# An attention segment on TensorE: four filler products per head group, with four later products brought forward and staged out of PSUM

## The chip, the cores and the metric

The kernel runs on one core of one Trainium2 chip. The metric is device time in microseconds (us) of one execution; a run's figure is the median of its executions. TensorE (PE) multiplies matrices and writes to PSUM, of which this program uses eight banks; ScalarE (ACT) computes exponentials and GELUs, VectorE (DVE) does elementwise work and statistics, GpSimd (POOL) the masks, and SyncE issues the transfers. The granted clock is the share of PE's full clock that the profile recorded as granted (1.00 on the pages of both kernels).

## The reference, cut to what matters

A pre-LayerNorm attention block with a compressive memory, followed by a gMLP block. 2048 tokens of width 1024, 32 heads of width 32, four segments of 512 tokens.

```python
for s in range(4):                                   # segments
    p = softmax(qs @ ks.T * scale + mask)            # causal, inside the segment
    o = g * (phi(qs) @ M) / (phi(qs) @ z) + (1 - g) * (p @ vs)
    M, z = M + phi(ks).T @ vs, z + phi(ks).sum()     # memory for the next segments
h = x + concat(o) @ wo
z1, z2 = split(gelu(layernorm(h) @ w_in))            # w_in: 1024 x 3584
out = h + (z1 * (w_sp @ layernorm(z2) + b_sp)) @ w_out
```

## The kernel before

The attention runs as 32 head groups (four heads each), eight per segment: groups 24 to 31 are the last segment. In each group the logits are computed in three rounds into PSUM banks 0 to 3, and each round's exponential (ScalarE) must have read those banks before the next round may overwrite them. PE would idle meanwhile, so it is given *fillers*: products with 512 columns, eight matmuls each, that belong to other work (projections of Q, K, V, the output projection of the segment before).

```python
logits(n, 0)                       # round 0 -> banks 0-3, exponential of 128x2048
fill(f1)
if n > 0:
    pv(n - 1, (0, 1) if split else (0, 1, 2, 3))   # probabilities of group n-1 times V
logits(n, 1)                       # round 1 -> banks 0-3, exponential of 128x2048
if n > 0:
    state(n - 1)                   # memory update; nothing to do in the last segment
bg_pop()
fill(f2)
if split:
    pv(n - 1, (2,))
logits(n, 2)                       # round 2, then mem(n), exponential of 128x1024, mem_norm(n)
...
fill(f3)
...
if split:
    pv(n - 1, (3,))                # and norm(n - 1) behind it
bg_pop()
fill(f4)
```

`mem(n)` multiplies with the memory and writes into the same four banks; `mem_norm(n)` (VectorE, writing `tm`) reads them, so the next group's first logits wait for it (0.61 us at the end of group 24). `norm(n)` (VectorE, `rd`, `ta`, `otok`) reads the PSUM of `pv(n)`, and `pv(n + 1)` waits for that (about 0.33 us in groups 29 and 30).

The last segment has fewer fillers of its own than the two before it, because it has no V of a next segment to compute:

```python
split = bool(s > 0 and c > 0 and not f4)
# last segment, c = n - 24:
if c < 4:
    f3 = [("v", s, c, 1)]
if c in (2, 3):
    f4 = [("wo", s - 1, 0, c - 2)]
elif c in (4, 5):
    f3 = [("wo", s - 1, 1, c - 4)]
elif c == 6:
    f3, f4 = [("wo", s - 1, 2, 0)], [("wo", s - 1, 2, 1)]
elif c == 7:
    f1, f2 = [("wo", s - 1, 3, 0)], [("wo", s - 1, 3, 1)]
    f3, f4 = [("z2", 0, 0)], [("z2", 0, 1)]
```

With f1 and f2 taken by the Q and K projections of the next group, groups 24, 25, 28 and 29 have three fillers and the others four. Behind the attention follow the w_in products for z2 (`z2_group(k, tc)`: eight matmuls of 448 columns, then a GELU), with the last segment's output projection (`wo(3, ...)`) among them.

The softmax here doesn't subtract the row's maximum and nothing guards it: scores larger than these inputs give would overflow.

Of the kernel before, what the change touches and what calls it, by code (L numbers as in the profile page):

```python
# [5 lines left out]
BF16 = mybir.dt.bfloat16  # L6
F32 = mybir.dt.float32
# [250 lines left out]
def bass_sequential_preLN__memory_aug_infini_attn__mixer_gmlp__prompt_kernel(  # L258
# [24 lines left out]
    def tens(name, shape, dt, off):  # L283
        sz = int(np.prod(shape[1:])) * mybir.dt.size(dt)
        assert off % 32 == 0 and off + sz <= ARENA, (name, off, sz)
        t = nc.alloc_sbuf_tensor_at(name, list(shape), dt, offset=abase + off)
        R.space[t[:].tensor.name] = ("sbuf", off)
        return t
# [32 lines left out]
    HNT = [tens("hnT0", [128, 8, L], BF16, 14 * K), tens("hnT1", [128, 8, L], BF16, 22 * K),  # L321
           tens("hnT2", [128, 8, L], BF16, 30 * K), tens("hnT3", [128, 8, L], BF16, 38 * K)]
    XNT = [tens("xnT0", [128, 8, L], BF16, 30 * K), tens("xnT1", [128, 8, L], BF16, 38 * K)]
    WV = tens("wv", [128, 8, D], BF16, 46 * K)
    WQ = tens("wq", [128, 8, D], BF16, 62 * K)
    WK = tens("wk", [128, 8, D], BF16, 78 * K)
    WO = tens("wo", [128, 8, D], BF16, 94 * K)
# [3 lines left out]
    LNO = [b1("lno%d" % i, [128, D], BF16) for i in range(3)]  # L331
    OT = b1("oT", [128, NQ, L], BF16)
    b2 = Bump(134 * K, ARENA)
    XCH = [b2("xch%d" % i, [128, D], BF16) for i in range(4)]
    QK = [b2("qk%d" % i, [128, 2, L], BF16) for i in range(2)]
    PQK = [b2("pqk%d" % i, [128, 2, L], BF16) for i in range(2)]
# [39 lines left out]
    def mm8(dst, lhs, rhs, n=8):  # L376
        for i in range(n):
            pe.matmul(dst, lhs(i), rhs(i), start=(i == 0), stop=(i == n - 1))
# [5 lines left out]
    def wcols(ap, lo, hi):  # L384
        return ap[:, lo:hi].rearrange("(c p) n -> p c n", p=128)

    for tc in range(4):
        x_load(tc)
    sp.dma_start(WV[:, :, 0:256], wcols(A_wv, 0, 256))
    sp.dma_start(WV[:, :, 256:512], wcols(A_wv, 256, 512))  # L390
    sp.dma_start(WK[:, :, 0:256], wcols(A_wk, 0, 256))
    sp.dma_start(WQ[:, :, 0:256], wcols(A_wq, 0, 256))
    sp.dma_start(BETAB[:], A_beta.partition_broadcast(128))
    sp.dma_start(WV[:, :, 512:1024], wcols(A_wv, 512, D))


    pool.memset(MHALF[:], -0.5)
# [69 lines left out]
    def proj_v_cols(s, tcl, lo, w):  # L467
        b = next_bank()
        xt = XNT[s % 2]
        mm8(PS[:, b, 0:w], lambda i: xt[:, i, tcl * 128:(tcl + 1) * 128], lambda i: WV[:, i, lo:lo + w])  # L470
        act.activation(V[:, tcl, lo // 32:(lo + w) // 32, 0:32],
                       PS[:, b, 0:w].rearrange("p (h d) -> p h d", d=32), ACTF.Copy)

# [14 lines left out]
    def phi_exp(n):  # L488
        q, p, e = phi_views(n)
        act.activation(e, q, ACTF.Exp)  # L490
# [27 lines left out]
        if rnd == 2 and n >= NQ:  # L518
            mem_norm(n)

    def pv(n, cqs):
        c = n % NQ
        for cq in cqs:
            for j in range(cq + 1):
                rnd, o = {0: (0, cq * 128), 1: (1, cq * 128 - 128), 2: (2, cq * 128 - 256), 3: (1, 384)}[j]
                for i in range(4):
                    pe.matmul(PVA[:, cq, i, :], E[n % 2][rnd][:, i, o:o + 128], V[:, j, 4 * c + i, 0:33],
                              start=(cq % 2 == 0 and j == 0 and i == 0), stop=False, skip_group_check=True)
        if 3 in cqs:
            norm(n)  # L530

    def mem(n):
        c = n % NQ
# [10 lines left out]
    def norm(n):  # L544
        s, c = divmod(n, NQ)
        ot = OTOK[s % 2][:, :, c * 128:(c + 1) * 128].rearrange("p q (i d) -> p q i d", d=32)
        dve.reciprocal(RD[:], PVA[:, :, :, 32])
        dve.tensor_tensor(RD[:], RD[:], OMG[:, c:c + 1, :].to_broadcast([128, 4, 4]), ALU.mult)
        rb = RD[:].unsqueeze(3).to_broadcast([128, 4, 4, 32])
        if s == 0:  # L550
            dve.tensor_tensor(ot, PVA[:, :, :, 0:32], rb, ALU.mult)
        else:
            dve.tensor_tensor(TA[:], PVA[:, :, :, 0:32], rb, ALU.mult)
            dve.tensor_tensor(ot, TA[:], TM[n % 2][:], ALU.add)
        if c == NQ - 1:
            for tcl in range(4):
                to_T(OT, tcl, OTOK[s % 2][:, tcl, :])
# [20 lines left out]
    def wo(s, tcl, half):  # L578
        tc = 4 * s + tcl
        if half == 0 and tcl < 3:  # L580
            xr_load(tc + 1)
        b = next_bank()
        mm8(bank(b), lambda i: OT[:, i, tcl * 128:(tcl + 1) * 128], lambda i: WO[:, i, half * 512:(half + 1) * 512])
        hs = slice(half * 512, (half + 1) * 512)
        dve.tensor_tensor(HCH[tc % 3][:, hs], XR[tc % 2][:, hs], bank(b), ALU.add)
        if half == 1:
            sp.dma_start(out2d[tc * 128:(tc + 1) * 128, :], HCH[tc % 3][:])
            ln_tasks(HCH[tc % 3], HNT[s], tcl)
# [6 lines left out]
    def bg_pop():  # L595
        if lnq[2]:
            src, dst, tcl, k = lnq[2].pop(0)
            to_T(dst, tcl, ln_apply(src, k))
        if lnq[1]:
            it = lnq[1].pop(0)  # L600
            ln_rstd(it[3])
            lnq[2].append(it)
        if lnq[0]:
            it = lnq[0].pop(0)
            lnq[1].append(it + (ln_stats(it[0]),))
# [51 lines left out]
    def win_load(k):  # L657
        kind, lo, w = CH[k]
        sp.dma_start(WIN[k % 3][:, :, 0:w], wcols(B_w_in, lo, lo + w))

    zs, zq = [], []

    def z2_group(k, tc):
        s, tcl = divmod(tc, 4)
        b = next_bank()
        wi = WIN[k % 3]
        mm8(PS[:, b, 0:448], lambda i: HNT[s][:, i, tcl * 128:(tcl + 1) * 128], lambda i: wi[:, i, 0:448])
        act.activation(Z2[:, tc, k * 448:(k + 1) * 448], PS[:, b, 0:448], ACTF.Gelu_apprx_tanh)
        zs.append((k, tc))

    def z2_stats():
# [14 lines left out]
    for n in range(LAST + 1):  # L686
        s, c = divmod(n, NQ)
        f1, f2, f3, f4 = [], [], [], []
        if n < LAST:
            f1, f2 = [("qk", n + 1, 1)], [("qk", n + 1, 0)]  # L690
        if s == 0:
            f3 = [("v", 0, c, 1)] if c < 4 else [("v", 1, c - 4, 0)]
        elif s < NSEG - 1:
            if c < 2:
                f3, f4 = [("v", s, 2 * c, 1)], [("v", s, 2 * c + 1, 1)]
            elif c < 6:
                f3, f4 = [("wo", s - 1, c - 2, 0)], [("wo", s - 1, c - 2, 1)]
            else:
                f3, f4 = [("v", s + 1, 2 * (c - 6), 0)], [("v", s + 1, 2 * (c - 6) + 1, 0)]
        else:  # L700
            if c < 4:
                f3 = [("v", s, c, 1)]
            if c in (2, 3):
                f4 = [("wo", s - 1, 0, c - 2)]
            elif c in (4, 5):
                f3 = [("wo", s - 1, 1, c - 4)]
            elif c == 6:
                f3, f4 = [("wo", s - 1, 2, 0)], [("wo", s - 1, 2, 1)]
            elif c == 7:
                f1, f2 = [("wo", s - 1, 3, 0)], [("wo", s - 1, 3, 1)]  # L710
                f3, f4 = [("z2", 0, 0)], [("z2", 0, 1)]

        def fill(lst):
            for u in lst:
                {"v": proj_v, "wo": wo, "qk": proj_qk, "z2": z2_group}[u[0]](*u[1:])

        if s < NSEG - 1 and c < 4:
            ln_tasks(XCH[c], XNT[(s + 1) % 2], c)
        if s < NSEG - 2 and c >= 4:
            x_load(4 * (s + 2) + c - 4)  # L720
        if s > 0 and c == 1:
            xr_load(4 * (s - 1))

        split = bool(s > 0 and c > 0 and not f4)
        logits(n, 0)
        fill(f1)
        if n > 0:
            pv(n - 1, (0, 1) if split else (0, 1, 2, 3))
        logits(n, 1)
        if n > 0:  # L730
            state(n - 1)
        bg_pop()
        fill(f2)
        if split:
            pv(n - 1, (2,))
        logits(n, 2)
        if n == 0:
            mask_g()
        if n < LAST:
            phi_exp(n + 1)  # L740
        fill(f3)
        if n < LAST:
            phi_max(n + 1)
        if split:
            pv(n - 1, (3,))
        bg_pop()
        fill(f4)
        bg_pop()
        if n == 1:
            sp.dma_start(WO[:], wcols(A_wo, 0, D))  # L750
        if n in (28, 29):
            win_load(n - 28)
    pv(LAST, (0, 1, 2, 3))
    xr_load(4 * (NSEG - 1))


    rot["banks"] = [6, 7, 0, 1, 2, 3, 4, 5]
    rot["n"] = 0
    win_load(2)

# [2 lines left out]
            r = tb * 512 + tcl * 128  # L763
            sp.dma_start_transpose(WSPT[tb % 2][:, :, tcl * 128:(tcl + 1) * 128], B_w_sp[r:r + 128, :])

    for k in range(4):
        for tc in range(2 if k == 0 else 0, NTC):
            z2_group(k, tc)
            if k == 0:
                bg_pop()  # L770
                if 5 <= tc < 9:
                    wo(NSEG - 1, tc - 5, 0)
                    bg_pop()
                    wo(NSEG - 1, tc - 5, 1)
                    bg_pop()
            z2_stats()
            if len(zq) > 1:
                z2_apply()
        if k + 3 < 8:
            win_load(k + 3)  # L780
        assert k == 0 or not any(lnq)
    while zs:
        z2_stats()
    for k in range(4, 8):
# [66 lines left out]
```

## Time and profile before

| | before |
|---|---|
| time, median | 806.98 us (806.93 to 807.08) |
| profiled span | 805.2 us |
| PE, DVE, ACT busy | 99%, 46%, 37% |
| granted clock | 1.00 |

From the page of the kernel before: the busy time of each engine, then PE and its clock in 40 slices (tenths busy), then the shares of the chain that ended last.

```profile
PE 796.1 (99%) x5407; PEld 384.7 (48%) x5407; DVE 368.7 (46%) x756; ACT 301.8 (37%) x356; POOL 121.5 (15%) x234
...
PE   8999999999999999999999999999999999999998
...
PEclk9999999999999999999999999999999999999999
...
PE 92%; DVE 5%; ACT 2%; issue 1%; DMA 0%
```

Only PE matters: it has 92% of the chain that ended last, and the other engines idle for more than half the time. What can be won is PE's own waiting. The page rounds that away ("99%", nines in every slice), so one goes to the timeline of PE. Its columns are start, time taken, engine, line, operation, output and inputs, shapes, count, and in brackets the idle time before it with the one that ended it. (All instructions have the line L209, that of a helper.) These lines are the first logits of each group (`32x512`), by whose starts a group's length is read, and the lines of the last segment with a wait for `tm` or `ta`:

```profile
235.98 0.39 PE L209 MATMUL ps<-qk_96 32*128 32x512 bf16 x4
...
244.50 0.40 PE L209 MATMUL ps<-qk_97 32*128 32x512 bf16 x4 [0.61 <-DVE tm_111 L209]
...
252.38 0.39 PE L209 MATMUL ps<-qk_96 32*128 32x512 bf16 x4 [0.22 <-DVE tm_112 L209]
...
261.93 0.39 PE L209 MATMUL ps<-qk_97 32*128 32x512 bf16 x4
...
271.49 0.40 PE L209 MATMUL ps<-qk_96 32*128 32x512 bf16 x4
...
279.36 0.40 PE L209 MATMUL ps<-qk_97 32*128 32x512 bf16 x4 [0.22 <-DVE tm_111 L209]
...
281.92 0.37 PE L209 MATMUL ps<-v,e_104 128*128 128x33 bf16 x8 [0.33 <-DVE ta L209]
...
287.75 0.39 PE L209 MATMUL ps<-qk_96 32*128 32x512 bf16 x4 [0.21 <-DVE tm_112 L209]
...
290.31 0.37 PE L209 MATMUL ps<-v,e_107 128*128 128x33 bf16 x8 [0.34 <-DVE ta L209]
...
297.81 0.39 PE L209 MATMUL ps<-qk_97 32*128 32x512 bf16 x4
```

Groups 26 and 27 (252.38 to 271.49, four fillers) take 9.55 and 9.56 us; their one wait, not shown, is 0.15 us for an exponential, and groups 30 and 31 have one such wait too. Group 24 (three fillers) ends in a 0.61 us wait for `tm`, the memory norm; groups 25, 28 and 29 in one of 0.21 or 0.22 us; in groups 29 and 30 PE also waits about 0.33 us for `ta`. The idle time in brackets is counted from the modelled end of the matmul before, so the time that PE really loses is a little more (for one wait after the change, 0.37 us in brackets and 0.53 us by the starts of the matmuls around it); lengths from start to start hold all of it.

The chain of waits of this kernel, cut to its end (start, time taken, what):

```profile
301.41 1.89 ACT e_108 L209
...
303.34 499.12 PE ps L209 x2430
```

From group 31's third logits on PE is never held up again: 499 us in one piece.

### The profile page before, as it was taken

What the parts mean: (1) busy time and instruction counts of PE and PEld (TensorE: products, weight loads), DVE (VectorE), ACT (ScalarE), POOL (GpSimd) and SP (SyncE); (2) the same over time, 40 slices, a digit from 0 to 9 for tenths busy, and PEclk for the clock granted to TensorE, in tenths of its full rate; (3) what the DMA queues carried; (4) which work ended last, traced back from release to release, by engine and by line L of the source; (5) the groups of instructions that cost most, each with busy time, mean ns of one, the idle gap of its engine ahead of it and who ended that gap; (6) DMA issues with size and microseconds to landing.
All of it is one profiled execution on the core that took longest, in us unless ns stands there. A gap on an engine that the chain in (4) does not pass through costs nothing.

```text
span 805.2 us, 12550 instructions
## 1 busy us (share of the span) xinstructions
PE 796.1 (99%) x5407; PEld 384.7 (48%) x5407; DVE 368.7 (46%) x756; ACT 301.8 (37%) x356; POOL 121.5 (15%) x234
## 2 busy tenths in 40 slices
PE   8999999999999999999999999999999999999998
PEld 4445544455444455455544444444444444444444
DVE  4653688669854585744463000054233324423332
ACT  3898876886778763233333333100000000000000
POOL 2342433233323231100131000000000000000000
PEclk9999999999999999999999999999999999999999
DMA  9782544455414057611115000550270044011002
GB/s 270 183 171 60 92 80 118 83 95 83 97 40 80 28 158 146 149 46 53 53 53 130 2 1 0 189 120 0 79 138 1 27 101 88 1 59 53 1 7 85
DMA packets 125992, 64.79 MB, mean 80 GB/s; under 512 B 94832, under 2 KB 114928, under 8 KB 125936
## 3 DMA queue, kind: packets, MB, share of 16 engines
q1 hardware_dynamic: 125936, 63.99, 34.1%
q8 instruction: 42, 0.69, 0.4%
q14 instruction: 14, 0.11, 0.1%
HBM read 32.51 MB, written 8.39 MB: 51 GB/s over the span
## 4 chain that ended last, share of the span: by engine, by line
PE 92%; DVE 5%; ACT 2%; issue 1%; DMA 0%
PE ps L209 92%; ACT e_105 L209 1%; DVE ta L209 1%; DVE stats_61 L209 0%; DVE stats_62 L209 0%; ACT e_108 L209 0%; DVE rdm L209 0%; DMA xch_92<-in_A_x_dram 0%; DVE hch_85 L209 0%; DVE rd L209 0%; ACT e_109 L209 0%; ACT e_106 L209 0%; DVE pqk_99 L209 0%; ACT e_104 L209 0%; DVE stats_59 L209 0%
## 5 line engine op out<-in xcount | busy, mean ns | idle before, releaser
L209 PE MATMUL ps<-w_out,yT 128*128 128x512 bf16 (+1 forms) x462 | 97.4, 373 | 0.0
L209 PE MATMUL ps<-wspT_121,z_119 128*128 128x512 bf16 x448 | 97.0, 379 | 0.0
L209 PE MATMUL ps<-wspT_122,z_119 128*128 128x512 bf16 x448 | 97.0, 379 | 0.0
L209 PEld LDWEIGHTS ps<-w_out,yT 128*128 128x128 bf16 x462 | 45.2, 98 | 51.7
L209 PEld LDWEIGHTS ps<-wspT_122,z_119 128*128 128x128 bf16 x448 | 43.8, 98 | 52.8
L209 PEld LDWEIGHTS ps<-wspT_121,z_119 128*128 128x128 bf16 x448 | 43.8, 98 | 52.9
L209 DVE TENSOR_TENSOR tmpg_128<-ps,brow_126 128x512 f32<-128x512 f32 x14 | 9.7, 691 | 117.1 <-DMA brow_126<-in_B_b_sp_dram 96.8
L209 ACT ACTIVATE z_119<-ps 128x448 bf16<-128x448 f32 x64 | 34.8, 544 | 75.1 <-PE ps L209 74.9
L209 PE MATMUL ps<-wo,oT 128*128 128x512 bf16 x256 | 58.4, 379 | 0.0
L209 ACT ACTIVATE z1T<-ps 128x512 bf16<-128x512 f32 x56 | 33.4, 597 | 63.3 <-PE ps L209 63.3
L209 DVE BATCH_NORM_STATS2 zst<-z_119 128x6 f32<-128x448 bf16 x64 | 39.1, 620 | 33.2 <-ACT z_119 L209 33.2
L209 PEld LDWEIGHTS ps<-wo,oT 128*128 128x128 bf16 x256 | 24.4, 98 | 27.4 <-issue 0.4
L209 ACT ACTIVATE e_107<-ps 128x2048 bf16<-128x2048 f32 x16 | 30.0, 1874 | 12.7 <-PE ps L209 12.7
L209 ACT ACTIVATE e_108<-ps 128x2048 bf16<-128x2048 f32 x16 | 30.0, 1877 | 10.7 <-PE ps L209 10.7
L209 ACT ACTIVATE e_104<-ps 128x2048 bf16<-128x2048 f32 x16 | 30.0, 1875 | 10.4 <-PE ps L209 10.4
L209 ACT ACTIVATE e_105<-ps 128x2048 bf16<-128x2048 f32 x16 | 30.0, 1877 | 9.8 <-PE ps L209 9.8
L209 PE MATMUL ps<-xnT_78,wk 128*128 128x512 bf16 x128 | 30.4, 380 | 0.0
L209 PE MATMUL ps<-xnT_77,wk 128*128 128x512 bf16 x128 | 30.4, 380 | 0.0
L209 PE MATMUL ps<-xnT_78,wq 128*128 128x512 bf16 x128 | 30.3, 379 | 0.0
L209 PE MATMUL ps<-xnT_77,wq 128*128 128x512 bf16 x128 | 30.2, 379 | 0.0
L209 PE MATMUL ps<-wv,xnT_77 128*128 128x512 bf16 (+1 forms) x160 | 29.9, 337 | 0.2 <-DMA wv<-in_A_wv_dram 0.2
L209 PE MATMUL ps<-wv,xnT_78 128*128 128x512 bf16 x128 | 29.6, 379 | 0.0
(218 smaller groups left out, 1171.6 us busy)
## 6 DMA issues: line engine op xcount, KB each, us to landing
w_out<-in_B_w_out_dram SPq DMA_DIRECT2D x1, 3584.0 KB, 12.7
wo<-in_A_wo_dram SPq DMA_DIRECT2D x1, 2048.0 KB, 9.9
xr_83<-in_A_x_dram SPq DMA_DIRECT2D x8, 256.0 KB, 3.3
xr_84<-in_A_x_dram SPq DMA_DIRECT2D x8, 256.0 KB, 3.9
win_116<-in_B_w_in_dram SPq DMA_DIRECT2D x2, 896.0 KB, 4.9
wk<-in_A_wk_dram SPq DMA_DIRECT2D x1, 1536.0 KB, 10.9
wq<-in_A_wq_dram SPq DMA_DIRECT2D x1, 1536.0 KB, 14.3
out_dram<-hch_85 SPq DMA_DIRECT2D x6, 256.0 KB, 3.0
```

The costliest lines, as they stand in the source:

```text
L209: ins = getattr(e, op.name)(*op.args, **op.kw)
```

## The change

The intent: give every group of the last segment four fillers. V and output-projection products are packed two to a group, as in the middle segments, which leaves group 30 without f3 and f4 and group 31 without f1 and f2. Into these go four w_in products from the stage behind the attention. Their GELUs would need another table of ScalarE's than the exponentials (in the timeline before, a table load of 1.28 us stands at 305.05 us between the last exponential and the first GELU), and their place in z2 is still taken by buffers of the attention, so the four leave PSUM as plain f32 copies in a staging buffer and get their GELU after the last exponential. To have w_in in time, the V weights are cut in two buffers, whose first is free earlier. The splitting of `pv`, made for groups with three fillers, goes.

```diff
+    ZSTG = [tens("zstg%d" % i, [128, 448], F32, (134 + 2 * i) * K) for i in range(4)]
...
+    def z2_group(k, tc, stage=None):
...
+        if stage is None:
+            z2_gelu(k, tc, PS[:, b, 0:448])
+        else:
+            act.activation(ZSTG[stage][:], PS[:, b, 0:448], ACTF.Copy)
+            staged.append((k, tc, ZSTG[stage][:]))
...
+        elif c < 2:
+            f3, f4 = [("v", s, 2 * c, 1)], [("v", s, 2 * c + 1, 1)]
+        elif c < 6:
+            f3, f4 = [("wo", s - 1, c - 2, 0)], [("wo", s - 1, c - 2, 1)]
+        elif c == 6:
+            f3, f4 = [("z2", 0, 4, 0)], [("z2", 0, 5, 1)]
         else:
...
+            f1, f2 = [("z2", 0, 6, 2)], [("z2", 0, 7, 3)]
+            f3, f4 = [("z2", 0, 0)], [("z2", 0, 1)]
...
         if n > 0:
-            pv(n - 1, (0, 1) if split else (0, 1, 2, 3))
+            pv(n - 1)
...
         if n < LAST:
             phi_exp(n + 1)
+        while n == LAST and staged:
+            z2_gelu(*staged.pop(0))
         fill(f3)
...
-        if n in (28, 29):
-            win_load(n - 28)
+        if n in (24, 26):
+            win_load((n - 24) // 2)
...
-    rot["banks"] = [6, 7, 0, 1, 2, 3, 4, 5]
+    rot["banks"] = [0, 1, 2, 3, 6, 7, 4, 5]
```

Left out: the V weights as two tensors, and the new order of the remaining w_in products with the last segment's output projection among them.

More of the change, by code (lines that the diff above doesn't have):

```diff
@@ L323, in bass_sequential_preLN__memory_aug_infini_attn__mixer_gmlp__prompt_kernel @@
     XNT = [tens("xnT0", [128, 8, L], BF16, 30 * K), tens("xnT1", [128, 8, L], BF16, 38 * K)]
-    WV = tens("wv", [128, 8, D], BF16, 46 * K)
+    WV = [tens("wv%d" % i, [128, 8, 512], BF16, (46 + 8 * i) * K) for i in range(2)]
     WQ = tens("wq", [128, 8, D], BF16, 62 * K)
@@ L388, in bass_sequential_preLN__memory_aug_infini_attn__mixer_gmlp__prompt_kernel @@
         x_load(tc)
-    sp.dma_start(WV[:, :, 0:256], wcols(A_wv, 0, 256))
-    sp.dma_start(WV[:, :, 256:512], wcols(A_wv, 256, 512))
+    sp.dma_start(WV[0][:, :, 0:256], wcols(A_wv, 0, 256))
+    sp.dma_start(WV[0][:, :, 256:512], wcols(A_wv, 256, 512))
     sp.dma_start(WK[:, :, 0:256], wcols(A_wk, 0, 256))
@@ L393, in bass_sequential_preLN__memory_aug_infini_attn__mixer_gmlp__prompt_kernel @@
     sp.dma_start(BETAB[:], A_beta.partition_broadcast(128))
-    sp.dma_start(WV[:, :, 512:1024], wcols(A_wv, 512, D))
+    sp.dma_start(WV[1][:], wcols(A_wv, 512, D))
     pool.memset(MHALF[:], -0.5)
@@ L469, in proj_v_cols @@
         xt = XNT[s % 2]
-        mm8(PS[:, b, 0:w], lambda i: xt[:, i, tcl * 128:(tcl + 1) * 128], lambda i: WV[:, i, lo:lo + w])
+        mm8(PS[:, b, 0:w], lambda i: xt[:, i, tcl * 128:(tcl + 1) * 128], lambda i: WV[lo // 512][:, i, lo % 512:lo % 512 + w])
         act.activation(V[:, tcl, lo // 32:(lo + w) // 32, 0:32],
@@ L519, in logits, with pv @@
             mem_norm(n)
-    def pv(n, cqs):
+    def pv(n):
         c = n % NQ
-        for cq in cqs:
+        for cq in range(4):
             for j in range(cq + 1):
@@ L528, in pv @@
                               start=(cq % 2 == 0 and j == 0 and i == 0), stop=False, skip_group_check=True)
-        if 3 in cqs:
-            norm(n)
+        norm(n)
     def mem(n):
@@ L659, in win_load @@
         sp.dma_start(WIN[k % 3][:, :, 0:w], wcols(B_w_in, lo, lo + w))
-    zs, zq = [], []
-    def z2_group(k, tc):
+    zs, zq, staged = [], [], []
+    def z2_group(k, tc, stage=None):
         s, tcl = divmod(tc, 4)
@@ L667, in z2_group, with z2_gelu @@
         mm8(PS[:, b, 0:448], lambda i: HNT[s][:, i, tcl * 128:(tcl + 1) * 128], lambda i: wi[:, i, 0:448])
-        act.activation(Z2[:, tc, k * 448:(k + 1) * 448], PS[:, b, 0:448], ACTF.Gelu_apprx_tanh)
+        if stage is None:
[3 more added lines that the diff above has]
+            staged.append((k, tc, ZSTG[stage][:]))
+    def z2_gelu(k, tc, src):
+        act.activation(Z2[:, tc, k * 448:(k + 1) * 448], src, ACTF.Gelu_apprx_tanh)
         zs.append((k, tc))
@@ L699, in bass_sequential_preLN__memory_aug_infini_attn__mixer_gmlp__prompt_kernel @@
                 f3, f4 = [("v", s + 1, 2 * (c - 6), 0)], [("v", s + 1, 2 * (c - 6) + 1, 0)]
-        else:
-            if c < 4:
-                f3 = [("v", s, c, 1)]
-            if c in (2, 3):
-                f4 = [("wo", s - 1, 0, c - 2)]
-            elif c in (4, 5):
-                f3 = [("wo", s - 1, 1, c - 4)]
-            elif c == 6:
-                f3, f4 = [("wo", s - 1, 2, 0)], [("wo", s - 1, 2, 1)]
-            elif c == 7:
-                f1, f2 = [("wo", s - 1, 3, 0)], [("wo", s - 1, 3, 1)]
-                f3, f4 = [("z2", 0, 0)], [("z2", 0, 1)]
+        elif c < 2:
[4 more added lines that the diff above has]
+            f3, f4 = [("z2", 0, 4, 0)], [("z2", 0, 5, 1)]
+        else:
+            f1, f2 = [("z2", 0, 6, 2)], [("z2", 0, 7, 3)]
+            f3, f4 = [("z2", 0, 0)], [("z2", 0, 1)]
         def fill(lst):
@@ L722, in bass_sequential_preLN__memory_aug_infini_attn__mixer_gmlp__prompt_kernel @@
             xr_load(4 * (s - 1))
-        split = bool(s > 0 and c > 0 and not f4)
         logits(n, 0)
@@ L733, in bass_sequential_preLN__memory_aug_infini_attn__mixer_gmlp__prompt_kernel @@
         fill(f2)
-        if split:
-            pv(n - 1, (2,))
         logits(n, 2)
@@ L743, in bass_sequential_preLN__memory_aug_infini_attn__mixer_gmlp__prompt_kernel @@
             phi_max(n + 1)
-        if split:
-            pv(n - 1, (3,))
         bg_pop()
@@ L750, in bass_sequential_preLN__memory_aug_infini_attn__mixer_gmlp__prompt_kernel @@
             sp.dma_start(WO[:], wcols(A_wo, 0, D))
-        if n in (28, 29):
-            win_load(n - 28)
-    pv(LAST, (0, 1, 2, 3))
+        if n in (24, 26):
+            win_load((n - 24) // 2)
+    pv(LAST)
     xr_load(4 * (NSEG - 1))
-    rot["banks"] = [6, 7, 0, 1, 2, 3, 4, 5]
+    rot["banks"] = [0, 1, 2, 3, 6, 7, 4, 5]
     rot["n"] = 0
@@ L764, in wsp_load @@
             sp.dma_start_transpose(WSPT[tb % 2][:, :, tcl * 128:(tcl + 1) * 128], B_w_sp[r:r + 128, :])
-    for k in range(4):
-        for tc in range(2 if k == 0 else 0, NTC):
-            z2_group(k, tc)
-            if k == 0:
-                bg_pop()
-                if 5 <= tc < 9:
-                    wo(NSEG - 1, tc - 5, 0)
-                    bg_pop()
-                    wo(NSEG - 1, tc - 5, 1)
-                    bg_pop()
-            z2_stats()
-            if len(zq) > 1:
-                z2_apply()
-        if k + 3 < 8:
-            win_load(k + 3)
-        assert k == 0 or not any(lnq)
+    todo = [(0, 2), (0, 3), (0, 8), (0, 9), 0, (0, 10), 1, (0, 11), 2, (1, 0), 3]
+    todo += [(1, tc) for tc in range(1, 4)] + [(0, tc) for tc in range(12, NTC)]
+    todo += [(1, tc) for tc in range(4, NTC)] + [(k, tc) for k in (2, 3) for tc in range(NTC)]
+    for it in todo:
+        if isinstance(it, int):
+            for half in range(2):
+                wo(NSEG - 1, it, half)
+                bg_pop()
+            continue
+        z2_group(*it)
+        bg_pop()
+        z2_stats()
+        if len(zs) > 1:
+            z2_stats()
+        if len(zq) > 1:
+            z2_apply()
+        if it[1] == NTC - 1:
+            win_load(it[0] + 3)
+    assert not any(lnq)
     while zs:
```

## The prediction

> **What bounds it now.** TensorE. The page gives PE 99% of an 805.2 us span, and the chain of waits is 92% PE; from 303.3 us on it is one unbroken piece of 499 us on PE. ScalarE is busy 37%, VectorE 46%, granted clock full. So only TensorE's idle time, or less TensorE work, can shorten the run. The change removes no product: it only moves four w_in groups forward into the last attention segment (head groups 24 to 31) and undoes the splitting of the probability-times-V products.
>
> **Where TensorE idles in that segment.** Timeline of PE, start of one head group to the next: groups with four fillers in segments 2 and 3 take 9.57 us (with the state products), in the last segment 9.55 us without them (groups 26, 27). The three-filler groups 24, 25, 28, 29 take 8.52, 7.88, 7.87, 8.39 us, and group 30 (four products, but behind a delayed norm) 10.06 us. One 512-column filler is 8 x 216 ns = 1.73 us, so against the dense 9.55/9.57 they waste 0.68 (group 24: PE waits 0.6 us for VectorE's tm, the memory norm), 0.05, 0.05, 0.56 and 0.50 us (29, 30: about 0.33 us waiting for VectorE's ta behind the late, split product). Sum 1.84 us. The rest of a group's non-product time (about 1.35 us by start-to-start intervals) is in every dense group too and stays: the 1.88 us exponential of 128x2048 must end before the next logits overwrite its banks.
>
> **After.** Groups 24 to 30: 9.57 + 6 x 9.55, minus 2 x 0.215 because group 30's two w_in fillers are 448 wide (1.51 us); group 31, to the end of its last product with V, 10.03 now, about 9.82 after: its first narrow filler saves 0.215, its second only lengthens the wait for the second exponential. Sum 76.3 us, of which 4 x 1.51 = 6.05 us is work taken from the later stage: 70.2 us against 71.9 us (235.98 to 307.84). Gain about 1.6 us.
>
> **What is added.** Four ScalarE copies and four GELUs from SBUF, some 0.54 us each as the present 128x448 GELU takes. [...] staging should force no table load; the trace agrees so far, copies and exponentials alternate with none between them, and one 1.28 us load stands at 305.05 us. Still one load after the change. The four late GELUs delay ScalarE about 2.2 us after the last exponential, but the next products go to banks 0 to 3, so banks 6 and 7 are wanted only 6 us later. ScalarE is slack there (busy 0.54 of 1.51 us). The output-projection products of the last segment start, as now, four groups (6.05 us) after the last product with V; the transposed OT chunk lands about 5.45 us after it now, so 0.6 us of slack stays. The last LayerNorm transposes land about 2 us before their w_in group. Earlier w_in loads: no wait.
>
> **Prediction:** 805.3 us, 8 in 10 between 804.6 and 806.4. Faster by over 2%: 0.01; within 2%: 0.98; slower by over 2%: 0.01.
>
> **Right if:** every head group from 24 to 30 takes 9.1 to 9.6 us; the PE waits for tm and ta in the last segment are gone, a wait of about 0.5 us before group 31's third logits remains; exactly one table load after the exponentials; PE unbroken from there, and that stage about 6 us shorter.
>
> **Wrong if:** a table load appears between exponentials (over 2.5 us each pair), OT's transposes arrive late for the first output projection, VectorE's backlog of statistics holds banks or the last LayerNorms, or the waits just move to the exponentials.

The sum: 76.3 us for the segment, less 6.05 us of moved work, against 71.9 us, so 1.6 us of gain. The trace before: copies and exponentials alternate there without a load between them.

## The result

805.37 us (805.27 to 805.38, 4 runs) against 806.98 us (806.93 to 807.08, 4 runs): 1.61 us less. The ratio is 0.998, 95% interval 0.9962 to 0.9997. A ratio here is the mean time of one kernel's runs over that of the other's runs of the same rounds, so it is not quite the ratio of the medians. Executions over 1.5% slower than the fastest of the same kernel are left out of the means.

The timeline of PE after the change, the same kind of lines (groups 24 to 26, then 30 and 31; groups 27 to 29 read as 25 and 26 do, each with the one 0.15 us wait):

```profile
236.07 0.39 PE L209 MATMUL ps<-qk_101 32*128 32x512 bf16 x4
...
245.64 0.40 PE L209 MATMUL ps<-qk_102 32*128 32x512 bf16 x4
...
251.18 0.29 PE L209 MATMUL ps<-qk_102 32*128 32x256 bf16 x4 [0.15 <-ACT e_113 L209]
...
255.19 0.39 PE L209 MATMUL ps<-qk_101 32*128 32x512 bf16 x4
...
293.41 0.39 PE L209 MATMUL ps<-qk_101 32*128 32x512 bf16 x4
...
298.94 0.29 PE L209 MATMUL ps<-qk_101 32*128 32x256 bf16 x4 [0.15 <-ACT e_110 L209]
...
302.53 0.39 PE L209 MATMUL ps<-qk_102 32*128 32x512 bf16 x4
...
307.85 0.29 PE L209 MATMUL ps<-qk_102 32*128 32x256 bf16 x4 [0.37 <-ACT e_113 L209]
```

All waits for `tm` and `ta` are gone. What is left is the wait of each group's third logits (`32x256`) for the second exponential, which is longer in group 31 because its filler there is only 448 columns wide (1.69 us in the timeline, against 1.90 us for one of 512 columns). Lengths by group, start to start, in us (group 31 to the end of its last product with V, at 307.84 before and 312.35 after):

| group | 24 | 25 | 26 | 27 | 28 | 29 | 30 | 31 | sum |
|---|---|---|---|---|---|---|---|---|---|
| before | 8.52 | 7.88 | 9.55 | 9.56 | 7.87 | 8.39 | 10.06 | 10.03 | 71.86 |
| after | 9.57 | 9.55 | 9.55 | 9.55 | 9.55 | 9.57 | 9.12 | 9.82 | 76.28 |

The segment grew by 4.42 us, and the stage behind it shrank by the four products that it no longer has to do. A pair of them takes 3.02 us from start to start in the timeline before, so four are 6.05 us. 6.05 - 4.42 = 1.63 us is the gain. The chain of waits after the change shows the other side:

```profile
305.92 1.89 ACT e_113 L209
...
307.85 493.07 PE ps L209 x2398
```

PE's last unbroken piece is 493.07 us instead of 499.12: 6.05 us and 32 matmuls shorter, and still unbroken. The new order of the remaining products was not tried alone, but with PE unbroken before and after, and shorter by just the products that were moved, it has no share in the gain. ScalarE's timeline at the end of the segment shows how the staged groups go:

```profile
308.52 1.02 ACT L209 ACTIVATE e_114<-ps 128x1024 bf16<-128x1024 f32 x1 [0.29 <-PE ps L209]
309.56 1.28 ACT L209 ACT_TABLE_LOAD   x1
310.85 0.58 ACT L209 ACTIVATE z_124<-zstg_93 128x448 bf16<-128x448 f32 x1
...
312.74 0.95 ACT L209 ACTIVATE z_124<-ps 128x448 bf16<-128x448 f32 x2
314.06 0.54 ACT L209 ACTIVATE z_124<-ps 128x448 bf16<-128x448 f32 x1 [0.37 <-PE ps L209]
```

One table load behind the last exponential, as before; ScalarE is behind PE until 313.7 us and has caught up by 314.06.

### The profile page after: what moved, and what is told of

Read it like the earlier page. It is cut to its first block, busy times and chain, and to the rows that moved or that the text cites. A ratio compares the mean times of both kernels' runs of the same rounds, so it can differ in the third digit from the quotient of the medians.

```text
span 803.7 us, 12539 instructions
## 1 busy us (share of the span) xinstructions
PE 795.0 (99%) x5407; PEld 384.0 (48%) x5407; DVE 367.8 (46%) x756; ACT 302.7 (38%) x360; POOL 120.5 (15%) x234
## 3 DMA queue, kind: packets, MB, share of 16 engines
HBM read 32.51 MB, written 8.39 MB: 51 GB/s over the span
## 4 chain that ended last, share of the span: by engine, by line
PE 94%; DVE 2%; ACT 2%; DMA 0%; issue 0%
PE ps L209 94%; ACT e_113 L209 1%; ACT e_110 L209 1%; DMA xch_97<-in_A_x_dram 0%; DVE stats_61 L209 0%; DVE stats_62 L209 0%; ACT e_109 L209 0%; DVE stats_59 L209 0%; DVE ta L209 0%; DVE otok_120 L209 0%; DVE hch_86 L209 0%; DVE stats_60 L209 0%; DVE pqk_104 L209 0%; DVE lno_90 L209 0%; DVE rd L209 0%
## 5 line engine op out<-in xcount | busy, mean ns | idle before, releaser
L209 ACT ACTIVATE z_124<-ps 128x448 bf16<-128x448 f32 x60 | 32.4, 542 | 69.5 <-PE ps L209 69.5
L209 DVE RECIPROCAL rd<-ps 128x16 f32<-128x16 f32 x32 | 7.8, 244 | 48.8 <-PE ps L209 48.8
L209 POOL TENSOR_SCALAR_AFFINE_SELECT e_113<-e_113 128x512 bf16<-128x512 bf16 x32 | 20.2, 653 | 38.7 <-ACT e_113 L209 38.7
```

The source lines that it names most:

```text
L209: ins = getattr(e, op.name)(*op.args, **op.kw)
```

## The experiments

The theory: the gain is PE's waiting taken away. Four fillers per group cover the waits for the memory norm, and the four early w_in products are what makes four fillers possible; staging and bank order keep ScalarE's extra work off PE's path. Rival A: the gain comes from taking back the split of `pv`, whose late part delayed the norm. Rival B: it comes from the layout, the earlier loads and the bank order. All kernels gave correct results.

| run | time, us (range, 5 runs) | before, same rounds | ratio, 95% interval |
|---|---|---|---|
| e1_unsplit | 807.93 (807.79 to 808.04) | 807.13 | 1.0011 (0.9997 to 1.0024) |
| e6_layout | 807.08 (806.97 to 807.21) | 807.13 | 1.0000 (0.9987 to 1.0012) |
| e2_no_early | 812.40 (811.80 to 813.37) | 807.13 | 1.0068 (1.0055 to 1.0080) |
| e4_banks67 | 806.74 (806.61 to 806.80) | 807.13 | 0.9995 (0.9983 to 1.0008) |
| e3_gelu_at_once | 810.88 (810.12 to 811.21) | 806.96 | 1.0047 (1.0033 to 1.0061) |
| e5_pvlate | 803.56 (803.52 to 803.75) | 806.96 | 0.9958 (0.9945 to 0.9970) |
| e7_pad | 803.19 (803.09 to 803.33) | 806.98 | 0.9953 (0.9939 to 0.9966) |
| after_again | 805.44 (4 runs, 805.25 to 805.50) | 806.98 | 0.9980 (0.9966 to 0.9993) |

For tenths of a us the intervals are wide; the spread of the runs (0.1 to 0.3 us in most kernels) and the traces decide there.

### Rival A: the unsplit products with V alone

```diff
-        split = bool(s > 0 and c > 0 and not f4)
+        split = False
```

> The kernel before, with the splitting of the products with V switched off and nothing else. Main theory (the four fillers pay, by covering the wait of the next group's first logits for the memory norm): the three-filler groups 25, 28, 29 grow from 7.88, 7.87, 8.39 us to about 8.5 us each, as the unsplit three-filler group 24 takes (8.52), group 30 falls from 10.06 to 9.55; together 0.9 us slower, about 807.9 us. Rival A (the gain came from taking back the split, whose late product delayed the norm): groups 29 and 30 lose their waits for ta and the others stay, about 1.0 us faster, 805.9 us.

Measured: 807.93 us, slower than before by 0.8 us. Its timeline of PE at the ends of groups 24 and 29 (those of 25 and 28 read alike), and the start of group 31:

```profile
244.57 0.40 PE L209 MATMUL ps<-qk 32*128 32x512 bf16 x4 [0.61 <-DVE tm L209]
...
289.20 0.39 PE L209 MATMUL ps<-qk 32*128 32x512 bf16 x4 [0.61 <-DVE tm L209]
...
298.75 0.39 PE L209 MATMUL ps<-qk 32*128 32x512 bf16 x4
```

Now every three-filler group ends in the 0.61 us wait, and takes 8.50 to 8.52 us; group 30 takes 9.55 us. The waits for `ta` are gone, as rival A says, but they were the price of something that paid more: the split kept 0.4 us of products for the gap before the next logits. Rival A falls as the cause of the whole. It has a share, though: group 30 goes from 10.06 to 9.55 us here with its fillers unchanged, so about 0.5 us of what the change wins lies in the undone split. In groups 25, 28 and 29, with three fillers, the split saved about 1.4 us in all; with four the gap is covered anyway, and the split can go.

### Rival B: layout, loads and banks alone

```diff
-    WV = tens("wv", [128, 8, D], BF16, 46 * K)
+    WV = [tens("wv%d" % i, [128, 8, 512], BF16, (46 + 8 * i) * K) for i in range(2)]
...
-        if n in (28, 29):
-            win_load(n - 28)
+        if n == 24:
+            win_load(0)
+        if n == 28:
+            win_load(1)
...
-    rot["banks"] = [6, 7, 0, 1, 2, 3, 4, 5]
+    rot["banks"] = [0, 1, 2, 3, 6, 7, 4, 5]
```

> The kernel before, with the change's other parts alone: the V weights as two tensors, w_in loaded earlier (after groups 24 and 28), banks in the new order; fillers and split as before. Main theory: none of these was waited for, 807.0 us, as before, within 0.2 us. Rival B (the gain came from these): about 805.4 us.

Measured: 807.08 us against 807.13 us, no difference; the eight groups have the lengths of the kernel before. Rival B falls: these parts make the change possible and are worth nothing by themselves.

### Without the four early w_in products

```diff
         elif c == 6:
-            f3, f4 = [("z2", 0, 4, 0)], [("z2", 0, 5, 1)]
+            pass
         else:
-            f1, f2 = [("z2", 0, 6, 2)], [("z2", 0, 7, 3)]
+            pass
             f3, f4 = [("z2", 0, 0)], [("z2", 0, 1)]
```

The four are done in the next stage instead, whose order was adapted.

> The kernel after, without its four early w_in groups: the V and output-projection fillers stay packed two per group in groups 24 to 29, group 30 has two fillers, group 31 only its last two; the four w_in groups run in the next stage. Main theory: group 30 takes about 8.5 us, because the next logits wait for the memory norm, and group 31 idles about 2.5 us under its two exponentials; 2.40 + 1.05 + 1.51 = about 5.0 us slower than after, about 810.3 us, slower than before too. Rivals A (unsplitting) and B (weight layout, earlier loads, bank order) have all of their parts in this kernel and expect about 805.4 us.

Measured: 812.40 us, 7.0 us slower than the kernel after, where 5.0 were expected. The direction is right and rules out again that either rival is the whole cause, but 2 us were missing from the sum. PE's timeline of groups 30 and 31:

```profile
301.92 0.39 PE L209 MATMUL ps<-qk 32*128 32x512 bf16 x4 [2.34 <-DVE tm L209]
...
304.30 0.61 PE L209 MATMUL ps<-qk 32*128 32x384 bf16 x8 [0.89 <-ACT e L209]
306.89 0.40 PE L209 MATMUL ps<-qk 32*128 32x256 bf16 x4 [1.98 <-ACT e L209]
...
307.64 4.55 PE L209 MATMUL ps<-win,hnT 128*128 128x448 bf16 x14
```

Group 30 takes 8.50 us, as expected (293.42 to 301.92), and the waits are those of the sum. What was not in it: the matmuls behind them are slow. The eight logits matmuls at 304.30 take 0.61 us, against 0.40 us elsewhere, and the 14 w_in matmuls from 307.64 us on take 4.55 us, against 2.81 us for as many in the kernel after (at 299.79 us): 1.74 us more. ScalarE's first GELU shows that most of it lies in the first eight of them: it waits for PE and starts 3.23 us after the first of the eight (307.64 to 310.87), where the same takes 1.71 us in the kernel after (312.35 to 314.06). The page of this run has an 8 in the clock's row:

```profile
PE   8999999999999988999999999999999999999998
...
PEclk9999999999999998999999999999999999999999
```

The mean granted clock of this execution is 0.996, where it was 1.000 in all four runs of the kernel after. The 1.52 us more for eight matmuls that usually take 1.51 us (half of the 3.02 us of a pair) come to about half speed in that stretch, an estimate from these two numbers. What lowered the clock is not shown; the slow matmuls stand behind waits of 2.34 and 0.89 us (see the end). So the four early products are worth more here than the idle time that they use: without them the run lost the waits of the sum and, behind them, most of 2 us in slow matmuls. The scatter of this kernel goes with the granted clock: 811.80 us at a mean of 0.996, 813.37 us at 0.993.

### GELU at once instead of staging

```diff
-            act.activation(ZSTG[stage][:], PS[:, b, 0:448], ACTF.Copy)
+            act.activation(ZSTG[stage][:], PS[:, b, 0:448], ACTF.Gelu_apprx_tanh)
...
-            z2_gelu(*staged.pop(0))
+            z2_gelu(*staged.pop(0), ACTF.Copy)
```

The result goes through the same staging buffer, because its place in z2 is still in use by the attention.

> The kernel after, but the four early w_in groups get their GELU as they leave PSUM and are only copied at the end (staging turned round; results the same up to one rounding). Main theory: the compiled program shows seven table loads from group 30 on in place of one; each 1.28 us load sits before an exponential or a GELU, the three exponentials of group 31 come about 1.4, 3.6 and 6.0 us later, and PE waits for them: about 4.8 us slower than after, 810.2 us (808.5 to 812). If staging were not needed, it would stay at 805.4 us.

Measured: 810.88 us, 5.5 us slower than the kernel after (4.8 expected, inside the stated range). ScalarE's timeline of groups 30 and 31:

```profile
301.27 1.28 ACT L209 ACT_TABLE_LOAD   x1
302.56 0.98 ACT L209 ACTIVATE zstg<-ps 128x448 f32<-128x448 f32 x2
303.55 1.28 ACT L209 ACT_TABLE_LOAD   x1
304.84 1.88 ACT L209 ACTIVATE e<-ps 128x2048 bf16<-128x2048 f32 x1
306.74 1.28 ACT L209 ACT_TABLE_LOAD   x1
308.03 0.55 ACT L209 ACTIVATE zstg<-ps 128x448 f32<-128x448 f32 x1
308.58 1.28 ACT L209 ACT_TABLE_LOAD   x1
...
```

In group 31 each GELU puts 0.55 us of work and two loads of 1.28 us between two exponentials; there are seven loads in all from 301.27 us on. PE waits 0.93 us for the first exponential of group 31 and 3.02 us for the second in its timeline. The 16 w_in matmuls behind that (at 312.56 us) take 4.20 us, against 3.19 us for 16 in the kernel after: 1.01 us more, which is enough for the 0.7 us that the sum lacked. The mean granted clock was 0.998 in four of the five executions; the one where it was 1.000 took 810.12 us, close to the 810.2 us of the sum. With the GELU at once the change would have lost 3.9 us instead of winning 1.6.

### The old order of banks

```diff
-    rot["banks"] = [0, 1, 2, 3, 6, 7, 4, 5]
+    rot["banks"] = [6, 7, 0, 1, 2, 3, 4, 5]
```

> The kernel after, with the old order of PSUM banks (6, 7, 0, 1, ...) behind the attention. Main theory: the first w_in group after the last product with V then needs bank 6, which its GELU frees only after the four staged GELUs, at about 313.3 us against 312.35 us: PE waits about 0.95 us once, so about 806.3 us. If ScalarE's backlog did not matter, it would stay at 805.4 us.

Measured: 806.74 us, 1.37 us slower than the kernel after: the wait is there, but longer than the 0.95 us expected. PE's timeline, and then ScalarE's:

```profile
313.73 6.23 PE L209 MATMUL ps<-win,hnT 128*128 128x448 bf16 x32 [1.24 <-ACT z L209]
```

```profile
312.72 0.95 ACT L209 ACTIVATE z<-ps 128x448 bf16<-128x448 f32 x2
```

PE starts again when the *second* of the two GELUs has ended (312.72 + 0.95 = 313.67), not the first. The expectation had taken the product (0, 0) to sit in bank 6; counting the bank requests of the program gives bank 7 for it and bank 6 for (0, 1). So the new bank order saves 1.37 us, most of the change's gain: with the old order it would have been 0.4 us (806.74 against 807.13).

### One step further: the last quarter of the products with V moved into the remaining wait

```diff
+        late = s == NSEG - 1 and c > 0
...
-            pv(n - 1)
+            pv(n - 1, (0, 1, 2) if late else (0, 1, 2, 3))
...
         fill(f2)
+        if late:
+            pv(n - 1, (3,))
         logits(n, 2)
```

> The kernel after, with one more idea: in groups 25 to 31 the last quarter of the products with V (0.4 us) is moved behind the second filler, into the wait of the third logits for the second exponential. Main theory (those waits are what is left, 0.22 us in each of groups 25 to 30 and 0.43 us in group 31): about 6 x 0.22 + 0.3 = 1.6 us faster than after, 803.8 us, the groups at 9.33 us. If the later norm holds up VectorE's memory norm, the wait comes back before the next group's first logits, and it stays at 805.4 us or gets slower.

Measured: 803.56 us, against 803.8 expected; groups 25 to 28 take 9.32 us each. The chain of waits from 230 us on has one piece of PE left:

```profile
229.79 569.43 PE ps L209 x3158
...
```

The last segment now has no wait that ends on another engine. That also confirms what was left after the change: the third logits waiting for the second exponential.

### And one wait in the middle segments

Groups 11, 13, 19 and 21 take 9.68 us where their neighbours take 9.57. `MZB`, the memory matrix in bf16, has 272 bytes per head group, and the program records dependencies in cells of 32 bytes (`GRAN = 32` in the kernel), so that a group's slice shares a cell with that of one neighbour.

```diff
-    MZB = cb("mzb", [128, NQ, 4, 34], BF16)
+    MZB = cb("mzb", [128, NQ, 4, 36], BF16)
```

> The late quarter of the products with V (e5_pvlate) and one padding: each head group's slice of the memory matrix (mzb) grows from 272 to 288 bytes, so that neighbouring slices share no 32-byte cell in which the program records its dependencies. Main theory: head groups 11, 13, 19, 21 take 9.68 instead of 9.57 us because their memory product waits for the update of its neighbour's slice; they fall to 9.57, 4 x 0.11 = 0.45 us, about 803.1 us. If the wait is for something else on VectorE, it stays at 803.6 us.

Measured: 803.19 us, against 803.1 expected, and against 803.56 for e5_pvlate (of another call; both calls' kernel before is at 806.96 to 806.98 us). All four groups take 9.57 or 9.58 us. Group 11's memory product and VectorE's update of its neighbour's slice, in the kernel after:

```profile
117.12 0.41 PE L209 MATMUL ps<-mzb,pqk_104 128*128 128x132 bf16 x4
```

```profile
116.76 0.30 DVE L209 TENSOR_TENSOR mzb<-msum,maskg 128x132 bf16<-128x132 f32 x1
```

and in e7_pad:

```profile
116.93 0.41 PE L209 MATMUL ps<-mzb,pqk 128*128 128x132 bf16 x4
```

```profile
116.70 0.30 DVE L209 TENSOR_TENSOR mzb<-msum,maskg 128x132 bf16<-128x132 f32 x1
```

After the change the product starts when the update is over (116.76 + 0.30 = 117.06); in e7_pad it starts before the update has ended (117.00). The wait was for data that the product does not read. This version, 803.19 us, beats both kernels: 3.8 us below before.

### The kernel after, once more

> The kernel after once more, so that it stands on the same chip and rounds as the next run: 805.4 us.

Measured: 805.44 us in four runs. The fifth execution took 1643.5 us; it was the one that was profiled, and is set aside here (see the end).

## Why the prediction was right

Predicted 805.3 us, measured 805.37.

- *What bounds it*: PE. Right. e3_gelu_at_once shows the other side: ScalarE is not the limit by its busy time (38% there), but PE waited 0.93 and 3.02 us for two delayed exponentials.
- *The waste per group*: 1.84 us to be won in groups 24, 25, 28, 29 and 30, 0.2 us given back in group 31. Right: groups 25 to 29 came to 9.55 to 9.57 us, group 24 to 9.57, group 30 to 9.12, group 31 to 9.82; segment 76.28 us against the 76.3 predicted. Of the 1.84 us, 1.06 lie in groups 29 and 30, where the waits for `ta` are; e1_unsplit shows that those of group 30 go with the split alone. The reason that this could be read off so closely is that groups with four fillers existed in the same trace.
- *No work is saved*: right; the later stage shrank by 6.05 us, the predicted 4 x 1.51 us.
- *One table load*: right (309.56 us, 1.28 us long; from the end of the last exponential at 309.54 us to the first GELU at 310.85 us it is 1.31 us with the load in it). The four staging copies, from 301.12 to 308.23 us, stand between exponentials without a load. e3_gelu_at_once shows what six more would have done.
- *ScalarE's late GELUs are out of the way thanks to banks 0 to 3*: right, and e4_banks67 shows that it mattered: 1.37 us. The prediction named it, but did not say how much hung on it.
- *The remaining wait before group 31's third logits, "about 0.5 us"*: right; 0.37 us in the timeline's brackets, 0.53 us by the starts of the matmuls around it (0.72 us apart, where 0.19 us is usual).
- *What was not foreseen* lies in the experiments alone: the expectations of e2_no_early and e3_gelu_at_once summed up the waits and left out the slow matmuls that were then measured behind them (1.74 us more for 14 w_in matmuls, 1.01 us more for 16), and that of e4_banks67 had the wrong bank.

## What to carry to other kernels

Where one engine is 99% busy, as PE was here, compare the repeats of its loop from start to start: the shortest one that does the same work says what the others waste, and the sum of that waste, not the amount of work moved, is what a rearrangement can win (1.84 us of waste here, for 1.61 us of gain and 6.05 us of work moved). Work brought forward to fill gaps needs its by-products (here a GELU with another table, and two PSUM banks held longer) kept out of the engine that sets the pace; copy out now and finish later, and let the next products go to other banks (5.5 us and 1.37 us hung on these two here). Look too for waits on data that an instruction does not read, which come from how coarsely a program records its dependencies (0.11 us in each of four groups here).

## What stays open

- When the clock goes down. In e2_no_early the slow matmuls begin at 304.30 us, behind waits of 2.34 and 0.89 us with PE at work from 301.92 to 303.42 us between them, and a third wait of 1.98 us follows. In e3_gelu_at_once they stand behind waits of 0.93 and 3.02 us (eight w_in matmuls between the two take the usual 1.69 us): the four matmuls with the memory at 312.14 us take 0.62 us, against 0.41 us in the kernel after. In one execution of e3_gelu_at_once the granted clock was 1.000. One wait of 1.24 us (e4_banks67) left it at 1.00. How long PE has to wait before the clock goes down, and what brings it back, these runs do not show.
- One execution of the kernel after took 1643.5 us (in after_again; a span of 1641.8 us), where the other four took 805.25 to 805.50 us. The record gives its mean granted clock as 1.0; it gives 1.0 for e5_pvlate and e7_pad too, whose pages have no clock row, so this does not rule out a lower clock. It was one execution out of all; its cause was not found.
